# Moving one block's second products behind the first six products of the next pair

## Chip, cores and metric

One core of one Trainium2 chip. The metric is the device time of one execution in microseconds; the kernel before has a median of 809.07 us over 3 runs (808.87 to 809.78).

## What is computed

Three stages, of which the change touches the last. Windowed attention gives x (1536 tokens x 512). A rational feed-forward layer turns it into x again (1536 x 512). Then four experts, each with 1024 hidden units, weighted per token:

```
p = domain_probs / (domain_probs.sum(-1, keepdims=True) + 1e-09)
out = np.zeros((N, D), dtype=np.float32)
for e in range(E):
    h = np.maximum(x @ w1[e], 0.0)
    out += p[:, e:e + 1] * (h @ w2[e])
```

Inputs and output are float32. The output must be close enough to the float32 reference that each product is made from a high and a low half of both factors: three matmuls (high x high, low x high, high x low) for one product.

## The kernel before

**Blocks and pairs.** The 1536 tokens are three blocks of 512. In the last block order they are called PA, PB and LONE (line 818); LONE is the third. The experts' 4 x 1024 hidden units are cut into 16 pairs of two 128-wide tiles, one pair per `Chunk` (line 1006). Each pair has first products (x times w1, up to the relu) and second products (the relu's result times w2, summed into the output).

**First products.** Pair 0 makes them directly: 12 matmuls for each block and tile (`direct`, line 1086). Every later pair makes the six results (three blocks, two tiles) out of 20 products of sums of weight tiles with sums of blocks, three matmuls of 128x512 each (`product`, line 1067, its matmuls at line 1074). The tables `FLOW` and `FLOW_LATE` (lines 63 and 73) list for a pair the order of its steps: `("P", i, bank)` adds product i into a PSUM bank, `("seed", a, b, sign)` has ScalarE copy bank a into a fresh bank b (line 1041), `("spare", a, name)` has ScalarE copy bank a to SBUF (line 327), `("plus", bank, name, sign)` has VectorE add or subtract it (line 1056), and `("gate", bank, tile, block)` takes the relu, with its high half on ScalarE (line 1109) and its low half on VectorE (line 1112). Pair 1 goes by `FLOW_LATE`, whose first steps are

```
    ("P", 18, 0), ("P", 12, 1), ("seed", 0, 2, 1), ("P", 5, 3), ("spare", 1, "A"), ("P", 0, 4), ("seed", 1, 5, 1),
    ("P", 1, 0), ("seed", 3, 6, 1), ("plus", 4, "A", 1), ("P", 7, 0), ("seed", 3, 7, -1), ("spare", 4, "B"),
```

So products 18, 1 and 7 all go into bank 0 (tag `h`), and between 18 and 1 the first seed has to read that bank.

**Second products.** `second` (line 1120) makes, for one pair and block, four groups of 6 matmuls (line 1134), each group in a PSUM bank of tag `acc`, of which there are 4. In pair 0 ScalarE takes each group out into `p`, times the token's probability (line 1152); in the others VectorE adds it to `p` (line 1154). The relu's result is the tile `g` for PA and PB and `gb` for LONE.

**What sets the order.** `emit` first writes down every operation with its engine, an estimate of its time, what it comes after and which buffers it takes or uses. `tick` (line 1209) hands out due times in the order in which `products` (line 1248) is called, and that gives TensorE's operations their place. `Plan.rank` passes due times back to the operations ahead of them, and `Plan.run` lists everything, engine by engine, by when an operation could start and by how late it may be. Each engine then carries out its own list in order, and waits on semaphores where the list says so. For VectorE and ScalarE the place around the change also holds the building of the right factors (`plan_rights`, line 876): sums of blocks (`combine`, line 856), their high halves on ScalarE (line 863) and low halves on VectorE (line 868), in tiles `y`, `z`, `tm`, `w`, `x`.

Before the change the calls at the end of this order are lines 1261 to 1263: pair 0's second products of PA, the direct products of LONE, second products of PB, second products of LONE; then for each later pair its 20 products and the second products of LONE, PB and PA.

Of the kernel before, what the change touches and what calls it, by code (L numbers as in the profile page):

```python
# [20 lines left out]
B, H, S, D, NM = 2, 8, 768, 64, 8  # L21
# [75 lines left out]
FLOWS = (FLOW, BANK, SPARE), (FLOW_LATE, BANK_LATE, SPARE_LATE)  # L97
# [200 lines left out]
def emit(ctx: ExitStack, tc: tile.TileContext, qk, v0, kv, q8, w64, w32, coef, prob, out):  # L298
# [519 lines left out]
    PA, PB, LONE = LAST  # L818
# [429 lines left out]
    def products(c, *todo):  # L1248
        for x in todo:
            chunks[c].order(tick, x)  # L1250

    def a_second():
        t2[ending.pop(0)] = tick(12 * MM)

    lone = ("F", LONE, 0), ("F", LONE, 1)
    for b in (PA, PB):
        for j in range(2):
            products(0, ("F", b, j))
            if ending:
                a_second()  # L1260
    products(0, ("S", PA), *lone, ("S", PB), ("S", LONE))
    for c in range(1, NC):
        products(c, *(x[:2] for x in FLOWS[c == 1][0] if x[0] == "P"), ("S", LONE), ("S", PB), ("S", PA))

    prs = Buf("tm", [128, NT // 128], F32)
    o_ident = add([("POOL", 1.0)], lambda: make_identity(nc, ident))
# [170 lines left out]
```

## Time and profile before

| what | value |
|---|---|
| median of 3 runs | 809.07 us |
| the profiled execution, own time | 810.07 us |
| its span (first to last instruction) | 808.3 us |
| mean granted TensorE clock | 0.997 of full speed |
| TensorE busy | 793.9 us (98%) |
| VectorE, ScalarE, GpSimd busy | 648.9, 487.5, 357.0 us |

The profile is one execution, taken by the hardware profiler. PE is TensorE's matmul, PEld its weight load (which overlaps with matmuls), DVE is VectorE, ACT ScalarE, POOL GpSimd, SPq the queue that issues DMAs. An engine's busy time counts its own instructions, without waits. In the timeline rows that follow each other with the same line and tiles are merged; the time in brackets is how long the engine was idle just before, and what ended it. A matmul's shown end is modelled and reaches over the next one's start, so pace is read from starts.

### The profile page before, as it was taken

How to read it: one execution, taken by the hardware profiler on the slowest of the kernel's cores; microseconds unless marked ns; L12 is line 12 of the kernel's file. 1: busy time of each engine (PE TensorE's matmuls, PEld its weight loads, DVE VectorE, ACT ScalarE, POOL GpSimd, SP SyncE). 2: the span in 40 equal slices, each digit the busy share in tenths (PEclk: the TensorE clock that was granted, in tenths of full speed). 3: DMA queues.
4: the chain of work that ended last, by engine and by line, in shares of the span. 5: the costliest groups of instructions: out<-in, count | busy, mean ns of one | idle time of the engine just before them, and what ended most of it. 6: DMA issues, size and time to landing. Idle time of an engine off the chain costs nothing.

```text
span 808.3 us, 11563 instructions
## 1 busy us (share of the span) xinstructions
PE 793.9 (98%) x4125; PEld 648.0 (80%) x4129; DVE 648.9 (80%) x1018; ACT 487.5 (60%) x1028; POOL 357.0 (44%) x384
## 2 busy tenths in 40 slices
PE   7999999999999999999999999999999999999998
PEld 4667788888888888878888888888888888888886
DVE  5898789999988788879869669669768768768655
ACT  6899878877778777565634534543643643643440
POOL 4698765555567466363434134124224224214100
PEclk9999999999999999999999999999999999999999
DMA  9986132212130100000111011011011001000004
GB/s 346 361 296 204 54 105 79 74 58 75 64 98 7 46 0 2 27 26 27 53 52 50 4 52 53 1 52 53 6 48 53 19 34 52 27 27 0 1 1 156
DMA packets 22057, 55.42 MB, mean 69 GB/s; under 512 B 3952, under 2 KB 4208, under 8 KB 22000
## 3 DMA queue, kind: packets, MB, share of 16 engines
q1 hardware_dynamic: 22000, 54.69, 19.8%
q8 instruction: 32, 0.52, 0.3%
q14 instruction: 25, 0.20, 0.1%
HBM read 51.54 MB, written 3.15 MB: 68 GB/s over the span
## 4 chain that ended last, share of the span: by engine, by line
PE 79%; DVE 8%; ACT 5%; DMA 3%; POOL 2%; issue 2%; SPq 0%; DVEq 0%; POOLq 0%; ACTq 0%
PE acc L1134 31%; PE acc L1074 10%; PE acc L788 10%; PE h L1074 10%; PE h L666 6%; PE att L666 5%; PE att L1074 5%; DMA w<-kv 2%; ACT w L506 2%; DVE ts L745 1%; DVE y L398 1%; DVE tm L733 1%; DMA w<-q 1%; DVE tm L737 1%; DMA w<-qk 1%
## 5 line engine op out<-in xcount | busy, mean ns | idle before, releaser
L1134 PE MATMUL acc<-w,g 128*128 128x512 f32 x762 | 175.5, 389 | 0.0
L1134 PEld LDWEIGHTS acc<-w,g 128*128 128x128 f32 x762 | 143.0, 188 | 29.7
L372 POOL TENSOR_TENSOR w<-stg,w 128x512 fp32r<-128x512 f32 x34 | 44.5, 1328 | 252.7 <-ACT w L327 252.7
L1154 DVE SCALAR_TENSOR_TENSOR p<-acc,pr,p 128x512 f32<-128x512 f32 x179 | 131.2, 744 | 27.8 <-PE acc L1134 25.6
L788 PE MATMUL acc<-g,w 128*128 128x512 f32 x576 | 141.7, 392 | 0.4 <-POOL w L372 0.3
L788 PEld LDWEIGHTS acc<-g,w 128*128 128x128 f32 x576 | 107.0, 188 | 23.7 <-POOL w L372 1.1
L666 PE MATMUL h<-x,w 128*128 128x512 f32 x384 | 95.1, 394 | 0.0
L764 POOL TENSOR_TENSOR ts<-ts,tu 128x512 f32<-128x512 f32 x48 | 63.7, 1328 | 64.5 <-ACT ts L753 63.8
L1134 PE MATMUL acc<-w,gb 128*128 128x512 f32 x384 | 90.2, 390 | 1.8 <-ACT p L1152 1.4
L1134 PEld LDWEIGHTS acc<-w,gb 128*128 128x128 f32 x384 | 71.9, 188 | 17.5 <-ACT p L1152 1.8
L666 PEld LDWEIGHTS h<-x,w 128*128 128x128 f32 x384 | 71.0, 188 | 15.0 <-DVE ts L745 0.2
L1041 ACT ACTIVATE att<-h 128x512 f32<-128x512 f32 x14 | 8.1, 582 | 99.6 <-PE h L1074 99.6
L666 PE MATMUL att<-x,w 128*128 128x512 f32 x264 | 63.4, 389 | 0.0
L1074 PE MATMUL h<-w 128*128 128x512 f32 x222 | 57.9, 390 | 0.0
L666 PEld LDWEIGHTS att<-x,w 128*128 128x128 f32 x264 | 49.6, 188 | 10.3
L863 ACT ACTIVATE w<-z 128x512 fp32r<-128x512 f32 (+1 forms) x45 | 26.8, 598 | 48.2 <-POOL z L856 39.1
L1056 DVE TENSOR_TENSOR att<-att,ts 128x512 f32<-128x512 f32 x45 | 31.5, 699 | 25.9 <-ACT ts L327 24.9
L1074 PE MATMUL acc<-x,w 128*128 128x512 f32 x189 | 50.4, 389 | 0.0
L372 POOL TENSOR_TENSOR w<-y,w 128x512 fp32r<-128x512 f32 x32 | 42.7, 1334 | 17.2 <-ACT w L327 16.3
L1056 DVE TENSOR_TENSOR acc<-acc,ts 128x512 f32<-128x512 f32 x17 | 11.9, 700 | 47.4 <-ACT acc L1041 44.5
L1074 PEld LDWEIGHTS h<-w 128*128 128x128 f32 x222 | 41.6, 188 | 9.0 <-ACT acc L1041 0.4
L372 POOL TENSOR_TENSOR g<-ts,g 128x512 fp32r<-128x512 f32 x28 | 41.2, 1472 | 12.4 <-ACT g L327 12.1
(187 smaller groups left out, 1569.7 us busy)
## 6 DMA issues: line engine op xcount, KB each, us to landing
stg<-w SPq DMA_DIRECT2D x64, 512.0 KB, 3.4
w<-kv SPq DMA_DIRECT2D x32, 256.0 KB, 5.5
w<-q SPq DMA_DIRECT2D x16, 256.0 KB, 5.5
w<-qk SPq DMA_DIRECT2D x8, 400.0 KB, 6.6
out<-p SPq DMA_DIRECT2D x11, 256.0 KB, 2.0
w<-v SPq DMA_DIRECT2D x8, 256.0 KB, 6.4
out<-p SPq DMA_DIRECT2D x2, 128.0 KB, 1.7
pr<-prob SPq DMA_DIRECT2D x1, 24.0 KB, 3.8
```

The source lines that it names most:

```text
L372: engines[op.eng].tensor_tensor(out=dst[:, 1], in0=src, in1=dst[:, 0].bitcast(F32), op=ALU.subtract)
L398: DVE.tensor_scalar(out=y.ap, in0=words(1), scalar1=3, scalar2=0x3FFFFFF8, op0=ALU.logical_shift_left, op1=ALU.bitwise_and,)
L506: ACT.activation(k(n), p1()[:, n * KB : (n + 1) * KB], AF.Exp, scale=SCALE, bias=nm()[:, n : n + 1], accum_out=sm()[:, n : n + 1],)
L666: PE.matmul(s.h.ap, left(a, k), xs[k].ap[:, b], start=(k == 0 and n == 0), stop=(k == KT - 1 and n == 2),)
L764: lambda: POOL.tensor_tensor(out=s.ap, in0=s.ap, in1=u.ap, op=ALU.mult), [ln], [s, u],
L788: PE.matmul(ps, wt[f].ap[:, 1, a, d * 128 : (d + 1) * 128], g.ap[:, b], start=start, stop=stop)
L863: [("ACT", 0.52 * cost)], lambda: ACT.activation(hi(), src(), AF.Copy),
L1041: lambda o, src=src, dst=dst, sign=x[3]: ACT.activation(dst.buf.ap, src.buf.ap, AF.Copy, scale=float(sign)),
L1056: lambda o, ps=ps, s=s, op=ADD if x[3] > 0 else SUB: DVE.tensor_tensor(out=ps.buf.ap, in0=ps.buf.ap, in1=s.buf.ap, op=op),
L1074: PE.matmul(ps.ap, left(a), right(b), start=fresh and n == 0, stop=n == 2, skip_group_check=True,)
L1134: PE.matmul(ps.ap, gs[j][0].ap[:, a, d * 128 : d * 128 + 128], V.ap[:, j, b], start=j == 0 and n == 0, stop=j == 1 and n == 2,)
L1154: DVE.scalar_tensor_tensor(out=y, in0=ps.ap, scalar=p, in1=y, op0=ALU.mult, op1=ALU.add)
```

## The change

Of pair 0's second products, those of LONE are no longer ordered ahead of pair 1's products, but behind the first six of them (18, 12, 5, 0, 1, 7). Nothing else is changed in the text; the other engines' lists are worked out anew from the due times.

```diff
-    products(0, ("S", PA), *lone, ("S", PB), ("S", LONE))
+    products(0, ("S", PA), *lone, ("S", PB))
     for c in range(1, NC):
-        products(c, *(x[:2] for x in FLOWS[c == 1][0] if x[0] == "P"), ("S", LONE), ("S", PB), ("S", PA))
+        firsts = [x[:2] for x in FLOWS[c == 1][0] if x[0] == "P"]
+        if c == 1:
+            products(c, *firsts[:6])
+            products(0, ("S", LONE))
+            firsts = firsts[6:]
+        products(c, *firsts, ("S", LONE), ("S", PB), ("S", PA))
```

TensorE's list where pair 0 ends and pair 1 begins, before (line 1134 are second products, `w,g` of PB, `w,gb` of LONE; line 1074 are pair 1's products):

```order
L1134 MATMUL acc<-w,g 128x512 x24
L1134 MATMUL acc<-w,gb 128x512 x24
L1074 MATMUL h<-w 128x512 x3
L1074 MATMUL acc<-x,w 128x512 x6
L1074 MATMUL h<-w 128x512 x6
L1074 MATMUL h<-x,w 128x512 x3
L1074 MATMUL acc<-x,w 128x512 x6
L1074 MATMUL acc<-w 128x512 x3
```

and with the change:

```order
L1134 MATMUL acc<-w,g 128x512 x24
L1074 MATMUL h<-w 128x512 x3
L1074 MATMUL acc<-x,w 128x512 x6
L1074 MATMUL h<-w 128x512 x6
L1074 MATMUL h<-x,w 128x512 x3
L1134 MATMUL acc<-w,gb 128x512 x12
L1074 MATMUL acc<-w 128x512 x3
L1134 MATMUL acc<-w,gb 128x512 x12
L1074 MATMUL acc<-x,w 128x512 x6
```

The 24 second products of LONE now stand behind 18 matmuls of pair 1, in two halves with product 9 (`acc<-w`) between them; 17 and 3 follow.

The six products in TensorE's changed list more closely, with buffer numbers and the engines waited for (`h_3731` is bank 0, products 18, 1 and 7; `h_3753` is product 0):

```order
L1074 MATMUL h_3731<-w_3465,w_3455 128x512 x3
L1074 MATMUL acc_3738<-x_2815,w_3239 128x512 [waits Activation_49]
L1074 MATMUL acc_3744<-x_2806,w_3239 128x512 [waits Activation_49]
L1074 MATMUL h_3753<-w_3501,w_3239 128x512 [waits DVE_49]
L1074 MATMUL h_3731<-w_3465,w_3455 128x512 [waits Activation_49]
L1074 MATMUL h_3731<-w_3465,w_3455 128x512 [waits Pool_49]
L1074 MATMUL h_3731<-x_3196,w_3455 128x512 x3
L1134 MATMUL acc_3772<-w_2878,gb_3664 128x512 x3
```

The first wait on `h_3731` is product 1's, for the first seed, ScalarE's line 1041.

ScalarE's list at the same place, before (line 863 are high halves of right factors, 1152 evictions of pair 0's second products, 1041 seeds):

```order
L863 ACTIVATE w<-y 128x512 [waits DVE_49]
L863 ACTIVATE x<-y 128x512 [waits DVE_49]
L1152 ACTIVATE p<-acc,pr 128x512 [waits PE_49]
L863 ACTIVATE x<-tm 128x512 [waits DVE_49,Activation_49]
L1152 ACTIVATE p<-acc,pr 128x512 [waits PE_49,Pool_49]
L863 ACTIVATE x<-z 128x512 [waits Activation_49] x2
L1152 ACTIVATE p<-acc,pr 128x512 [waits PE_49] x3
L1041 ACTIVATE acc<-h 128x512 [waits PE_49,Activation_49]
```

and with the change:

```order
L863 ACTIVATE w<-y 128x512 [waits DVE_49]
L863 ACTIVATE x<-y 128x512 [waits DVE_49]
L1152 ACTIVATE p<-acc,pr 128x512 [waits PE_49]
L863 ACTIVATE x<-tm 128x512 [waits DVE_49,Activation_49]
L1041 ACTIVATE acc<-h 128x512 [waits PE_49,Activation_49]
L327 ACTIVATE ts<-acc 128x512 [waits PE_49]
L1041 ACTIVATE att<-acc 128x512 [waits PE_49]
L863 ACTIVATE x<-z 128x512 x2
L327 ACTIVATE tm<-h 128x512 [waits DVE_49]
L1152 ACTIVATE p<-acc,pr 128x512 [waits PE_49,Pool_49]
```

The first seed, `acc<-h`, moves forward from behind all of LONE's evictions to the place behind `x<-tm`; the three high halves and the eviction ahead of it keep their places. On VectorE one addition to `h` (line 1056) moves ahead of two low halves (line 868). GpSimd's and the DMA queue's lists stay as they were.

## Rows read from the trace of the kernel before

**Rows 1.** The page's busy time, share of the span and instructions of each engine.

```profile
PE 793.9 (98%) x4125; PEld 648.0 (80%) x4129; DVE 648.9 (80%) x1018; ACT 487.5 (60%) x1028; POOL 357.0 (44%) x384
```

**Rows 2.** Timeline of TensorE, 342 to 370: start us, length us, what [idle before].

```profile
342.07 5.60 PE L1134 MATMUL acc<-w,g 128*128 128x512 f32 x24
347.51 1.29 PE L1134 MATMUL acc<-w,gb 128*128 128x512 f32 x5
349.24 3.25 PE L1134 MATMUL acc<-w,gb 128*128 128x512 f32 x13 [0.43 <-DVE gb L1112]
353.85 1.66 PE L1134 MATMUL acc<-w,gb 128*128 128x512 f32 x6 [1.37 <-ACT p L1152]
...
357.41 1.77 PE L1074 MATMUL h<-w 128*128 128x512 f32 x6
359.01 0.85 PE L1074 MATMUL h<-x,w 128*128 128x512 f32 x3
...
369.25 3.11 PE L1134 MATMUL acc<-w,gb 128*128 128x512 f32 x13
```

**Rows 3.** Windows: stretch, length, busy PE, PEld, DVE, ACT, POOL, clock, DMA.

```profile
348.00:354.00 6.00, 4.20 (x18) 2.86 (x17) 6.00 (x8) 2.04 (x4) 4.01 (x4) 1.00 0.28 87
369.25:803.00 433.75, 433.75 (x1915) 359.18 (x1914) 329.24 (x490) 197.70 (x369) 129.22 (x150) 1.00 0.11 36
```

**Rows 4.** Chain of waits, 340 to 375: start us, us, what.

```profile
349.19 3.38 DVE y L856 x3
```

**Rows 5.** Timeline of ScalarE, 351 to 358.

```profile
351.45 0.63 ACT L863 ACTIVATE w<-y 128x512 fp32r<-128x512 f32 x1 [4.41 <-DVE y L856]
352.59 0.63 ACT L863 ACTIVATE x<-y 128x512 fp32r<-128x512 f32 x1 [0.51 <-DVE y L856]
353.13 0.67 ACT L1152 ACTIVATE p<-acc,pr 128x512 f32<-128x512 f32 x1
353.70 0.62 ACT L863 ACTIVATE x<-tm 128x512 fp32r<-128x512 f32 x1
354.22 0.68 ACT L1152 ACTIVATE p<-acc,pr 128x512 f32<-128x512 f32 x1
...
357.54 0.61 ACT L1041 ACTIVATE acc<-h 128x512 f32<-128x512 f32 x1
```

**Rows 6.** Timelines of VectorE and GpSimd, 349 to 377.

```profile
349.11 2.31 DVE L856 TENSOR_TENSOR y<-p 128x512 f32<-128x512 f32 x2
351.34 1.22 DVE L856 TENSOR_TENSOR y<-y,p 128x512 f32<-128x512 f32 x1
352.48 0.68 DVE L856 TENSOR_TENSOR tm<-tm,y 128x512 f32<-128x512 f32 x1
...
349.68 2.33 POOL L856 TENSOR_TENSOR z<-stg 128x256 f32<-128x256 f32 x2
...
376.44 1.30 POOL L868 TENSOR_TENSOR w<-z,w 128x512 fp32r<-128x512 f32 x1 [16.45 <-ACT w L863]
```

**Rows 7.** Timeline of TensorE's weight loads, at 358.

```profile
358.21 0.53 PEld L1074 LDWEIGHTS h<-w 128*128 128x128 f32 x3 [0.38 <-ACT acc L1041]
```

**Rows 8.** Windows of 1 us around the two falls of the clock.

```profile
7.00:8.00 1.00, 0.00 (x0) 0.00 (x0) 0.00 (x0) 0.51 (x1) 0.43 (x2) 1.00 0.98 373
8.00:9.00 1.00, 0.83 (x16) 0.79 (x16) 0.39 (x1) 1.00 (x8) 0.40 (x1) 0.71 1.04 409
9.00:10.00 1.00, 1.00 (x19) 0.90 (x16) 0.84 (x3) 1.00 (x8) 0.76 (x5) 0.50 1.02 402
...
11.00:12.00 1.00, 0.82 (x6) 0.44 (x7) 0.48 (x2) 1.00 (x8) 0.92 (x3) 0.59 1.02 410
...
807.00:808.00 1.00, 0.00 (x0) 0.00 (x0) 0.00 (x0) 0.00 (x0) 0.00 (x0) 0.57 0.00 0
```

**Rows 9.** Timeline of TensorE, at 8 and at 803.

```profile
8.17 0.95 PE L490 MATMUL att<-w 128*64 128x64 f32 x16 [1.55 <-ACT w L327]
...
803.08 1.59 PE L1178 MATMUL acc<-w,g 128*128 128x256 f32 x12
```

## The prediction

> **What bounds the kernel.** I read the page first: TensorE is busy 793.9 of 808.3 us, 98% [rows 1], and no other engine is over 80%. So the time is TensorE's matmuls plus the few places where it stands still, and a change of order can only move that standing still. The timeline of TensorE comes next [rows 2]. From 342.07 to 347.51 twenty-four matmuls start 5.44 us apart, so one starts every 0.2267 us. The 24 second products of the third block follow (the row of 347.51 to that of 353.85), then 60 matmuls of the second pair's products, and at 369.25 the next second products. That is 84 matmuls, 84 x 0.2267 = 19.04 us, in 21.74 us: 2.70 us are lost here. Where: five matmuls from 347.51 end their turn at 348.64, the next starts at 349.24 (0.60 us, a wait for VectorE's low half of gb); thirteen from there end theirs at 352.19, the next starts at 353.85 (1.66 us, a wait for ScalarE's eviction); six from 357.41 take 1.60 us instead of 1.36 (0.24 us). The other 0.20 us is spread thin, most of it a slower first step after each stop. Behind that, from 369.25 to 803, TensorE is busy 433.75 of 433.75 us [rows 3]: whatever is won or lost before 369.25 arrives at the end in full.
>
> The chain of waits says who made TensorE stand still: three sums on VectorE, 3.38 us together [rows 4], end at 352.57. ScalarE's rows show how they get to TensorE [rows 5]: ScalarE takes its instructions in the order in which they stand; it stood idle 4.41 us before the copy at 351.45, then began a second copy only at 352.59, when the sums were done; the eviction that TensorE wanted stands behind it and begins at 353.13. So ScalarE was stuck behind VectorE, and the eviction was merely the first thing in its queue that TensorE needed.
>
> **The change, part by part.**
>
> Removed: TensorE no longer asks for the low half of gb at 348.64 nor for the eviction at 352.19. Both stops go, 0.60 + 1.66 us. The low half is ready at 349.2 and the new place needs it far later, so it costs nothing there.
>
> Moved forward: products 18, 12, 5 and 0, twelve matmuls, run from 347.51 to 347.51 + 2.72 = 350.23. What they need is old: their operands were used or made earlier, and the two acc banks come from the evictions that ran before 347.04 (ScalarE is idle for the 4.41 us ahead of 351.45 [rows 5]).
>
> Added: the fifth product, 1, goes into the bank of product 18, and may do so only when ScalarE has copied that bank into the seed of another. In ScalarE's new order this seed stands behind both copies, the eviction and a third copy. None of these four is touched by the change, and what they wait for is VectorE's sums, which don't wait for TensorE's place either: two sums from 349.11 (2.31 us), one from 351.34 (1.22 us), the last from 352.48 (0.68 us) [rows 6]. So they run as before: 351.45, 352.59, 353.13, 353.70, and the seed takes the place at 354.22 where an eviction stood [rows 5]. Before, the seed began at 357.54 [rows 5] and TensorE's weight load for product 1 began at 358.21 [rows 7], 0.67 us later. The same step now gives 354.22 + 0.67 = 354.89. TensorE stands from 350.23 to 354.89: 4.66 us. Four products do not reach across ScalarE's blockade, and the second products that could have filled it (thirteen ran in it before) now stand behind product 1 in TensorE's order.
>
> The rest, 72 matmuls, needs 72 x 0.2267 = 16.32 us. I looked for the next late one. The second of the four groups wants a bank whose last reader is ScalarE's third item behind the seed, done near 356.4, at 357.7; the third group wants a seed behind its first eviction, some 0.6 us to spare; product 17 wants the eviction of the third group, some 0.4 us to spare. All are counted in steps of 0.5 to 0.6 us per ScalarE item, from one start to the next [rows 5], so no second stop, or one of under 0.5 us. With 0.2 us of slow steps as before, 4.66 + 0.20 = 4.86 us are lost, against 2.70: **+2.2 us**.
>
> The clock: this is the term with no row for exactly this case. In the stretch of the old stops the granted clock stayed at 1.00, that is 2.4 GHz [rows 3], with TensorE working between stops of 0.60 and 1.66 us. But the trace has two falls to 0.50, 1.2 GHz [rows 8]. The first: TensorE did nothing from 7 to 8, restarted at 8.17 [rows 9], and the mean of 0.71 from 8 to 9 puts the fall at 8.42. The second: the last matmuls end at 803.08 + 1.59 = 804.67 [rows 9], and the mean of 0.57 from 807 to 808 puts the fall at 807.14, 2.47 us later. The new idle stretch, from the end of the last matmul at about 350.4 to 354.89, is 4.5 us: longer than the idle time ahead of either fall. So I expect one. Its length: low from 8.42 to the middle of 11 to 12 (0.59, so 11.82), 3.40 us [rows 8]; while low, half the work is done. Earliest, 2.47 us into the idle: low from 352.9 to 356.3, of which 1.4 us lie behind the restart, cost 0.7 us. Latest, 0.25 us after the restart as at 8.42: all 3.40 us at half pace, cost 1.7 us. No fall costs 0. I take the middle of the two ends with a fall, **+1.2 us**, and keep 0 and 1.7 for the range.
>
> The rule that bears on this is in the Trainium skill, "TensorE: Matmul & The Clock Gate", section "HAM oscillation — how this bites in real kernels": waits between bursts of matmuls let the clock drop, and each next burst starts slow. By the old stops' rows alone the sum would be +2.2 us; by that rule it is +3.4 us. The two falls in this trace agree with it.
>
> Moved with it, at no cost: on VectorE one addition to h goes ahead of two low halves, which are wanted by products 10 and 16, some forty matmuls (9 us) later; GpSimd's next sums wait for them and start about 1.3 us later, but GpSimd stands idle for 16.45 us behind them [rows 6]. Nothing on the DMA queues moves.
>
> Sum: 2.2 + 1.2 = +3.4 us. The profiled execution took 810.07 us with a span of 808.3, so it would take 813.5; it stands 1.0 us over the median, and on the median of 809.07 the same sum gives **812.5 us**. About 0.2%, 1.6 us, can be told from no change here.
>
> **The rivals.**
> - *The clock holds*: 809.07 + 2.2 = 811.3 us. For it: 1.00 through both old stops. Against it: a fall after 2.47 us of idleness. Chance 0.20.
> - *The other side, the products cover the blockade*: ScalarE makes the seed in its idle 4.41 us. Both old stops and the 0.24 us vanish, with their slow steps 2.7 us: 806.4 us. It decides at about 352.0: a seed that begins 2.2 us before 354.22 leaves the time as it was, an earlier one wins. Right behind the first copy (351.45 + 0.52) would be just even, so the seed must stand ahead of all four. The new order of ScalarE puts it behind them. Chance 0.04.
> - *The blockade is shorter*: if VectorE's three sums took 0.68 us each as the one at 352.48 does, not 1.22 as beside GpSimd's work from 349.68 [rows 6], ScalarE would be free 3 x 0.54 = 1.6 us earlier, and the sum would be +0.6 us without a fall: 809.7 us, no change that can be told. But GpSimd's part in this doesn't move. Chance 0.05.
> - *It gets worse*: a second stop of 0.5 us and a clock that stays low for twice as long (another 1.7 us), because TensorE's restart falls into the low time: near 814.7 us. Chance 0.06.
> - That the change does nothing can be left out: TensorE's new order has the second products moved, only with product 9 between their halves.
>
> **How the numbers follow.** The forecast keeps 0.65, and its own range is 811.9 to 813.0 (fall at its earliest or latest). A range of 8 in 10 takes in the case without a fall and a little scatter of the median, 811.0 to 813.3, and leaves out the second, third and fourth rival, 0.15. Faster by over 0.2%: the second rival, 0.04. Within 0.2%: the third, 0.05, and 0.03 of the first, whose 2.2 us is only 0.6 over the bound: 0.08. Slower: 0.88.
>
> **What the profile would show.** Right: twelve matmuls of L1074 from 347.5, then one stop near 350.2 to 354.9 put down to ScalarE's L1041, the seed near 354.2 just behind a copy of L863, no stop at gb or at L1152, and second products at L1134 from about 356. A granted clock under 1.00 in a few us around 355 shows the clock term, 1.00 throughout refutes it. Wrong: the seed before 352, a stop of under 2.7 us, or a time up to 809.

## The result, and the profile after

The changed kernel takes 813.8 us (median of 6 runs, 812.65 to 814.7), the kernel before 809.01 us beside it (6 runs, 808.8 to 810.62): a ratio of 1.0054, 95% interval 1.0041 to 1.0067. It is slower, and lies 0.5 us above the range of the prediction. The profiled execution took 814.43 us with a span of 812.7 us, 4.4 us more than before; the mean clock is 0.994 where it was 0.997.

The page shows hardly anything: TensorE has the same instructions as in [rows 1] and is busy 1.6 us longer: an instruction at a lower clock counts as busy for longer.

```profile
PE 795.5 (98%) x4125; PEld 650.2 (80%) x4129; DVE 649.2 (80%) x1018; ACT 488.0 (60%) x1028; POOL 355.7 (44%) x384
```

TensorE's timeline in the changed kernel, as in [rows 2] (start us, length us, what, idle before):

```profile
347.27 0.84 PE L1074 MATMUL h<-w 128*128 128x512 f32 x3
347.95 1.52 PE L1074 MATMUL acc<-x,w 128*128 128x512 f32 x6
349.31 0.84 PE L1074 MATMUL h<-w 128*128 128x512 f32 x3
354.60 1.65 PE L1074 MATMUL h<-w 128*128 128x512 f32 x3 [4.45 <-ACT acc L1041]
356.05 1.48 PE L1074 MATMUL h<-x,w 128*128 128x512 f32 x3
357.33 4.18 PE L1134 MATMUL acc<-w,gb 128*128 128x512 f32 x12
361.35 0.85 PE L1074 MATMUL acc<-w 128*128 128x512 f32 x3
...
373.60 2.65 PE L1134 MATMUL acc<-w,gb 128*128 128x512 f32 x11
```

Twelve matmuls (products 18, 12, 5, 0) start from 347.27 on; the turn of the last would end at 347.27 + 12 x 0.2267 = 349.99. Product 1 starts at 354.60. That is one stop of 4.61 us, put down to ScalarE's seed at L1041. Both old stops of [rows 2] are gone. Then something new: from 354.60 to 361.35 stand 18 matmuls, which need 18 x 0.2267 = 4.08 us and take 6.75. They lose 2.67 us without any idle time between them. The 84 matmuls from 347.27 to 373.60 take 26.33 us, 7.29 more than 19.04, and 4.61 + 2.67 is nearly all of it. Before, the same 84 took 21.74 us: 4.59 us less. (The profiled program came to this place 0.24 us earlier than before; its span is 4.4 us longer.)

ScalarE's timeline of the changed kernel shows the queue that made the stop, as in [rows 5]:

```profile
351.20 0.63 ACT L863 ACTIVATE w<-y 128x512 fp32r<-128x512 f32 x1 [4.40 <-DVE y L856]
352.34 0.63 ACT L863 ACTIVATE x<-y 128x512 fp32r<-128x512 f32 x1 [0.50 <-DVE y L856]
352.87 0.67 ACT L1152 ACTIVATE p<-acc,pr 128x512 f32<-128x512 f32 x1
353.44 0.62 ACT L863 ACTIVATE x<-tm 128x512 fp32r<-128x512 f32 x1
353.96 0.58 ACT L1041 ACTIVATE acc<-h 128x512 f32<-128x512 f32 x1
```

The seed could run from about 348 on, when product 18 is in its bank (in an experiment below it begins 0.94 us after the stretch does). ScalarE is idle then, but its list has four other instructions ahead of the seed, and the first waits for VectorE. The chain of waits of the changed kernel has the same three sums as [rows 4], and the seed behind them:

```profile
348.94 3.38 DVE y L856 x3
...
354.06 0.50 ACT acc L1041
```

Why the 18 matmuls lose 2.67 us is in the windows of the changed kernel (columns as in [rows 3]: busy PE, PEld, DVE, ACT, POOL, then the clock):

```profile
353.00:354.00 1.00, 0.00 (x0) 0.00 (x0) 1.00 (x2) 1.00 (x3) 0.00 (x0) 0.60 0.00 0
...
355.00:358.00 3.00, 3.00 (x8) 2.32 (x8) 2.00 (x3) 2.58 (x6) 0.62 (x1) 0.50 0.00 0
358.00:360.00 2.00, 2.00 (x6) 1.52 (x6) 0.00 (x0) 0.00 (x0) 2.00 (x4) 0.50 0.01 4
360.00:361.00 1.00, 1.00 (x6) 0.82 (x5) 0.00 (x0) 0.78 (x2) 1.00 (x3) 0.99 0.00 0
373.60:807.00 433.40, 433.40 (x1914) 358.87 (x1913) 330.34 (x490) 197.82 (x369) 127.98 (x150) 1.00 0.11 36
```

The mean of 0.60 from 353 to 354 is 0.80 us at 0.50 and 0.20 at 1.00, so the clock fell to 1.2 GHz at 353.20, inside the stop, and came back to 2.4 GHz near 360.02 (0.99): 6.82 us of low clock, of which 5.4 lie behind the restart. From 373.60 on TensorE is busy without a gap, so all of it arrives at the end.

### The profile page after: what moved, and what is told of

Same layout as the page of the kernel before. It is cut to its first block, busy times and chain, and to the rows that moved or that the text cites. A ratio compares the mean times of both kernels' runs of the same rounds, so it can differ in the third digit from the quotient of the medians.

```text
span 812.7 us, 11560 instructions
## 1 busy us (share of the span) xinstructions
PE 795.5 (98%) x4125; PEld 650.2 (80%) x4129; DVE 649.2 (80%) x1018; ACT 488.0 (60%) x1028; POOL 355.7 (44%) x384
## 4 chain that ended last, share of the span: by engine, by line
PE 86%; DVE 5%; ACT 4%; POOL 2%; DMA 2%; issue 1%; SPq 0%; DVEq 0%; POOLq 0%; ACTq 0%
PE acc L1134 32%; PE acc L788 13%; PE acc L1074 10%; PE h L1074 10%; PE h L666 8%; PE att L666 7%; PE att L1074 5%; ACT w L506 1%; DMA w<-qk 1%; POOL w L519 1%; DVE y L404 1%; DVE y L410 1%; DMA w<-q 1%; POOL ts L764 0%; ACT w L327 0%
## 5 line engine op out<-in xcount | busy, mean ns | idle before, releaser
L1041 ACT ACTIVATE att<-h 128x512 f32<-128x512 f32 x14 | 8.1, 582 | 99.7 <-PE h L1074 99.7
L863 ACT ACTIVATE w<-z 128x512 fp32r<-128x512 f32 (+1 forms) x45 | 26.8, 599 | 48.1 <-POOL z L856 39.1
```

Source lines behind the costliest of these rows:

```text
L863: [("ACT", 0.52 * cost)], lambda: ACT.activation(hi(), src(), AF.Copy),
```

## The experiments

The first question was how the loss divides between stop and clock, the second what sets the length of the low clock, the third whether ScalarE's order is the cause. Line numbers move by some lines in edited kernels: 1074 becomes 1078, 1084 or 1087, L1041 becomes L1051 or L1054, L863 becomes L864, 1134 becomes 1138, 1144 or 1147, 1152 becomes 1156 or 1162. All medians stand beside the kernel before on the same chip.

**The clock by itself: eighteen matmuls in the stop.** Between products 0 and 1 TensorE makes matmuls into a free bank that nobody reads.

```diff
+                    if c == 1 and x[1] == 0:
+                        keep = bank("att")
...
+                            for _ in range(BUSY):
+                                PE.matmul(keep.ap, left(0), right(0), start=True, stop=True)
```

> The changed kernel with 18 extra matmuls of 128x512 into a free bank between products 0 and 1, so that TensorE works through most of its stop (18 x 0.2267 = 4.1 of 4.5 us); their result is never read. Theory (ScalarE's blockade stops TensorE, and the long idleness then costs clock): the wait for the seed stays, the clock stays at 1.00 around 350 to 360, and the time is the changed kernel's less its clock cost of 2.6 us, about 811.1 us. Rival (the clock is a by-product and what costs is the second products' new place, with their bank waits): the time stays near 813.8, and stops show among the second products.

Measured: 813.22 us against 810.04 us, ratio 1.0033 (1.0020 to 1.0045). By the ratios, 1.0054 and this one, that is 1.7 us less than the changed kernel; expected were 2.6. The stop is filled, and the clock stays up. The timeline of TensorE, then a window:

```profile
350.39 4.24 PE L1044 MATMUL att<-w 128*128 128x512 f32 x18
355.02 0.96 PE L1084 MATMUL h<-w 128*128 128x512 f32 x3 [0.39 <-ACT acc L1051]
...
356.51 3.20 PE L1144 MATMUL acc<-w,gb 128*128 128x512 f32 x12
359.55 0.84 PE L1084 MATMUL acc<-w 128*128 128x512 f32 x3
```

```profile
350.00:361.00 11.00, 10.61 (x46) 8.13 (x45) 7.61 (x10) 7.85 (x14) 5.59 (x8) 1.00 0.14 48
```

Product 1 still waits until the seed is made, so the wait costs the same. Its 18 matmuls now take 355.02 to 359.55, 4.53 us, 0.45 over 4.08: 0.13 at the first step and 0.32 among the twelve second products. So of the 2.67 us that these 18 lost in the changed kernel, 0.45 are lost with the clock up too. The stretch of 84 takes 347.67 to 371.79, 24.12 us. So in the profiles the wait alone costs 24.12 - 21.74 = 2.4 us, and the clock 26.33 - 24.12 = 2.2 us more.

The same kernel was run again beside the changed kernel on one chip:

> The run with 18 extra matmuls in the stop, repeated beside the changed kernel. Theory: the clock holds at 1.00 in the stretch and the time is 1.7 to 2.6 us less than the changed kernel's. Rival (the clock costs nothing there): the same time as the changed kernel.

> The changed kernel, on the same chip as the other two and timed in the same rounds. Theory: about 4.5 us over the kernel before; in its profile one stop of 4.4 to 4.5 us and a low clock that begins inside it.

Measured: 812.62 us with the eighteen matmuls (1.0024, 1.0015 to 1.0032), 814.46 us for the changed kernel (1.0050, 1.0036 to 1.0064), against 810.84 us before. The clock costs 1.8 us in the medians, 2.1 by the ratios. On this chip the changed kernel is 3.6 us slower in the medians (4.1 by the ratio) and not 4.8; its profile has the same stop (4.45 us of idle time), the same low time (6.83 us) and a stretch of 26.22 us. A further profile of the changed kernel has them too:

> The changed kernel once more, for a second profile. Theory: the same stop of 4.4 to 4.5 us behind product 0; the clock falls again, for a time that need not be the 6.83 us of the first profile, and the time differs from 814.4 by half of the difference in low time that TensorE worked in.

Measured: 814.5 us, span 812.7, 4.44 us of idle time, a clock that is low from 353.41 to 360.24.

**Half as many.** The same edit with nine matmuls.

> As the run with 18 extra matmuls, with 9: TensorE works 2.04 us of its stop and then stands idle for about 2.4 us until the seed. Theory: the stop is as long; whether the clock falls is open. If it holds at 1.00, 811.1 us; if it falls as in the changed kernel, about 813.7 us.

Measured: 813.03 us, 1.0040 (1.0026 to 1.0054). TensorE's timeline, then the windows:

```profile
353.97 0.97 PE L1084 MATMUL h<-w 128*128 128x512 f32 x3 [2.44 <-ACT acc L1051]
```

```profile
355.00:356.00 1.00, 1.00 (x5) 0.81 (x4) 0.75 (x2) 1.00 (x3) 0.17 (x1) 0.74 0.00 0
356.00:358.00 2.00, 2.00 (x7) 1.51 (x5) 1.10 (x1) 0.95 (x2) 1.31 (x3) 0.50 0.00 0
358.00:359.00 1.00, 1.00 (x4) 0.80 (x3) 0.00 (x0) 0.69 (x1) 1.00 (x2) 0.55 0.02 8
```

The nine matmuls begin at 349.33 and take 2.20 us. Behind a stop of 2.44 us the clock fell too, but 1.5 us after the restart, at 355.48. It lasted 0.52 + 2 + 0.90 = 3.42 us, half of the changed kernel's. Either the shorter stop or the work during the low time could be the reason; the next two runs part these.

**The same idle time, with and without work behind it.** The unneeded matmuls wait for a copy of ScalarE, so the idle time is in front of them: eight in one kernel, three in the other.

```diff
+    listed.remove(dummy[1])
+    listed.insert(max(map(listed.index, (rights[11][2][0], dummy[0]))) + 1, dummy[1])
```

> The changed kernel, with eight matmuls that are not needed between products 0 and 1, as in the run with nine, but these read the copy that ScalarE begins at 352.3, so they start near 353.0: TensorE stands about 3.0 us, works 1.8 us (twice that at the lower clock), and begins product 1 with hardly a stop more. In the run with nine the idle time came behind them (2.44 us), the clock fell 1.5 us after the restart and was low for 3.41 us; in the changed kernel it fell inside the stop and was low for 6.83 us. Theory: what counts is whether TensorE works while the clock falls and after. Then a fall behind 353.0 is followed by 3.4 us of low clock (cost 1.7 us at most), and the time lies 0.9 us or more under the changed kernel's. Rival: the length of the idle time ahead counts, and 3.0 us is nearer to the changed kernel's 4.45: low for 6.83 us, and the time is that of the changed kernel or above it. No fall at all, with the time of the run with eighteen (1.8 us under the changed kernel), would refute both.

> The same with three matmuls instead of eight, from near 353.0 to 353.7: TensorE stands about 3.0 us, works 0.7 us, and stands another 1.0 to 1.3 us before product 1. By the theory that work while the clock falls makes the low time short, this is in between: 3.4 us if the fall comes while the three or product 1 run, 6.83 us if it comes in the second idle piece. By the rival (the idle time ahead counts) it is as in the run with eight. The stop ahead of product 1 ends at the same time in both, near 354.6 to 355.0.

Measured: with eight 813.88 us, 1.0041 (1.0026 to 1.0056); with three 815.02 us, 1.0052 (1.0036 to 1.0068). TensorE's timeline and windows with eight:

```profile
353.18 3.67 PE L1044 MATMUL att<-x,w 128*128 128x512 f32 x8 [2.87 <-ACT x L864]
356.69 0.85 PE L1084 MATMUL h<-w 128*128 128x512 f32 x3
```

```profile
353.00:354.00 1.00, 0.82 (x2) 0.73 (x3) 1.00 (x3) 1.00 (x3) 0.00 (x0) 0.58 0.00 0
...
356.00:357.00 1.00, 1.00 (x5) 0.82 (x4) 0.75 (x2) 1.00 (x3) 0.38 (x1) 0.71 0.00 0
```

and with three:

```profile
353.42 0.96 PE L1044 MATMUL att<-x,w 128*128 128x512 f32 x3 [2.87 <-ACT x L864]
355.00 1.65 PE L1084 MATMUL h<-w 128*128 128x512 f32 x3 [0.62 <-ACT acc L1051]
```

```profile
354.00:355.00 1.00, 0.38 (x2) 0.00 (x0) 1.00 (x2) 1.00 (x3) 0.00 (x0) 0.66 0.00 0
...
361.00:362.00 1.00, 1.00 (x5) 0.77 (x5) 0.00 (x0) 0.86 (x2) 0.01 (x1) 0.93 0.00 0
```

The idle time is 2.87 us in both. With eight the clock falls at 353.16, just as TensorE restarts, TensorE then works without a gap, and the clock is low for 0.84 + 2 + 0.58 = 3.42 us. With three it falls at 354.32; TensorE stands until 355.00 (0.62 us of idle time), and the clock is low for 0.68 + 6 + 0.14 = 6.82 us. So the idle time ahead did not decide it, and the rival falls: in this stretch the low time was 3.42 us with work all through it and 6.82 us with a stop reaching into it, in one profile each. In the medians the two kernels can't be told apart, as their intervals overlap; the stretches, 25.59 and 26.65 us (to the next second products at 373.01 and 374.32), differ by 1.1 us. The run with eight is only 0.7 us under the changed kernel's 26.33, expected were 0.9 or more: its unneeded matmuls ran at the low clock and held product 1 up until 356.69.

The falls near 8 us, where the first one of [rows 8] stands, don't keep to this. Thirteen of the fourteen profiles have one there, eleven of 3.4 us and two of 6.8, most of their matmuls being smaller ones of 128x64. Two of the runs below contradict each other in it. In the one with four products ahead the clock fell at 7.50, TensorE restarted only at 8.11, and the low time ended at 10.92, after 3.42 us:

```profile
8.11 1.12 PE L490 MATMUL att<-w 128*64 128x64 f32 x16 [2.06 <-ACT w L327]
```

```profile
7.00:8.00 1.00, 0.00 (x0) 0.00 (x0) 0.00 (x0) 0.56 (x2) 0.43 (x2) 0.75 0.98 357
...
10.00:11.00 1.00, 1.00 (x5) 0.22 (x4) 0.51 (x2) 1.00 (x9) 0.92 (x4) 0.54 1.03 410
```

In the one with ScalarE's order alone and TensorE's order of before, TensorE had restarted at 8.27, the clock fell at 9.02 and stayed low until 15.84, 6.82 us, though TensorE stood for only about 0.4 us of it:

```profile
8.27 0.69 PE L490 MATMUL att<-w 128*64 128x64 f32 x16 [1.28 <-ACT w L327]
```

```profile
9.00:10.00 1.00, 0.81 (x16) 0.81 (x16) 0.80 (x4) 1.00 (x9) 0.74 (x4) 0.51 1.02 403
...
15.00:16.00 1.00, 1.00 (x16) 0.67 (x17) 0.51 (x2) 1.00 (x7) 0.97 (x2) 0.58 1.13 428
```

So standing in the low time is not by itself what makes it 6.82 us; what decides between the two lengths in general stays open.

**VectorE's sums shorter.** A tiny GpSimd instruction that reads a late copy holds GpSimd's two sums back, so that they no longer run beside VectorE's.

```diff
+            for y in (a1, a2):
+                y.after.append(tiny)
+                tiny.next.append(y)
```

> The changed kernel, with GpSimd's two sums of 128x256 that run beside VectorE's y sums (349.5 to 351.8) held back until ScalarE's copy x<-tm is made, by a tiny GpSimd instruction that reads that copy. Theory: the y sums take about 0.7 instead of 1.2 us each, ScalarE's copy begins some 1.1 us earlier, the seed with it, and TensorE's stop shrinks from 4.45 to about 3.3 us: at least 1.1 us less than the changed kernel, 812.7 us or, if the clock falls for less time, down to 810.1. Rival (the sums are slow for another reason): 813.8 us, y sums as before.

Measured: 813.54 us, 1.0036 (1.0023 to 1.0049). VectorE's timeline, then TensorE's:

```profile
348.82 1.77 DVE L857 TENSOR_TENSOR y<-p 128x512 f32<-128x512 f32 x2
350.52 0.68 DVE L857 TENSOR_TENSOR y<-y,p 128x512 f32<-128x512 f32 x1
351.13 0.68 DVE L857 TENSOR_TENSOR tm<-tm,y 128x512 f32<-128x512 f32 x1
```

```profile
353.50 1.65 PE L1087 MATMUL h<-w 128*128 128x512 f32 x3 [3.39 <-ACT acc L1054]
```

The sums of 2.31 and 1.22 us in [rows 6] take 1.77 and 0.68 (the first two still begin beside a GpSimd instruction of line 372), ScalarE comes free 1.1 us earlier, and the stop is 1.1 us shorter: the length of ScalarE's blockade is VectorE's sums, as the prediction had it. The clock falls in this stop too and is low for 6.83 us, from 352.68 to 359.51. The stretch takes 25.54 us, 0.8 less than the changed kernel's; the ratio is 1.0036 where the changed kernel has 1.0050 and 1.0054, and the intervals overlap.

**The change with four products ahead instead of six.** Product 1 comes behind the second products again.

```diff
-            products(c, *firsts[:6])
+            products(c, *firsts[:4])
```

> The change with four products moved ahead instead of six: 18, 12, 5, 0, then all second products of the third block, then product 1. Theory: TensorE gets one group of 6 further before it needs the eviction behind ScalarE's blockade, stops near 351.4 until about 353.6, and has one or two short stops behind; idle stretches stay under 2.5 us, the clock stays at 1.00; near 810.3 us, between the kernel before and the changed one. Rival (the second products' place alone): as the changed kernel, near 813.8.

Measured: 812.54 us, 1.0031 (1.0020 to 1.0043): 2.5 us over the 810.04 us beside it, expected were 1.3. The single stop becomes two:

```profile
353.56 1.66 PE L1134 MATMUL acc<-w,gb 128*128 128x512 f32 x6 [2.10 <-ACT p L1152]
357.08 3.02 PE L1134 MATMUL acc<-w,gb 128*128 128x512 f32 x12 [1.86 <-ACT acc L1041]
```

The first waits for the eviction behind the same two copies, the second for a seed further back in the same queue (356.43). The stretch takes 347.21 to 370.82, 23.61 us, 1.87 more than before. In this profile (811.64 us) the clock stayed at 1.00 through both. Other executions had mean clocks down to 0.989 (814.83 us), so a fall there can't be ruled out for them.

**ScalarE's order alone, with the order before.** TensorE's list is that of before; the three copies go behind PB's last eviction.

```diff
+            for i in (13, 11, 15):
+                rights[i][2][0].after.append(o_done[PB, KT - 1])
```

> The kernel before, with TensorE's order as it was, but on ScalarE the last eviction of the second block's second products (line 1152) stands ahead of the copies that wait for VectorE's sums. Theory (ScalarE's order, not TensorE's, makes the stop of 1.66 us): that stop goes, the one of 0.60 us for gb stays, product 1 may wait up to 0.7 us for its seed: 807.3 to 807.8 us. Rival (the stop belongs to the place of the second products in TensorE's order): no change, 809.0 us.

Measured: 809.51 us, 0.9988 (0.9979 to 0.9997). The stop of 1.66 us in [rows 2] is gone, but a smaller one opens at product 1:

```profile
358.01 0.97 PE L1074 MATMUL h<-w 128*128 128x512 f32 x3 [0.60 <-ACT acc L1041]
```

The stretch (348.34 to 369.03) takes 20.69 us, 1.05 less than before. The medians differ by 0.5 us (810.04 to 809.51), the ratio gives 1.0; expected were 1.2 to 1.7.

**ScalarE's order alone, with the changed order.** TensorE's list is that of the change; the three copies go behind the first seed.

```diff
+                    if c == 1 and x[2] == 2:
+                        for i in (13, 11, 15):
+                            rights[i][2][0].after.append(o)
```

> The changed kernel, with TensorE's order as it is, but on ScalarE the three copies of right factors (lines 863: w<-y, x<-y, x<-tm) stand behind the first seed instead of ahead of it. Theory (blockade): the seed is ready near 349, product 1 follows product 0 without a stop, all three stops of the kernel before are gone and no fall of the clock follows: 809.0 - 2.7 = about 806.4 us. Rival (the second products' new place costs by itself): slower than the kernel before by at least 1 us, with a stop that ScalarE's order does not move.

Measured: 808.49 us, 0.9980 (0.9971 to 0.9989). Product 1 no longer waits at all. The gain over the kernel before is 1.6 us, expected were 2.6, since the third group of second products now waits for its seed. ScalarE's timeline, then TensorE's:

```profile
347.37 0.58 ACT L1041 ACTIVATE acc<-h 128x512 f32<-128x512 f32 x1
...
353.70 0.67 ACT L1156 ACTIVATE p<-acc,pr 128x512 f32<-128x512 f32 x1
354.40 0.58 ACT L1041 ACTIVATE acc<-acc 128x512 f32<-128x512 f32 x1
```

```profile
355.04 3.02 PE L1138 MATMUL acc<-w,gb 128*128 128x512 f32 x12 [0.97 <-ACT acc L1041]
```

That seed has an eviction ahead of it, and both stand behind the five copies.

**All of ScalarE's copies behind what TensorE waits for.** To the last edit it adds two: the copies also go behind the first eviction of the second products and the seed that follows it, and one spare copy behind the second eviction.

```diff
+            for i in (13, 11, 15, 10, 16):
+                for o in (out0, self_seed[0]):
+                    rights[i][2][0].after.append(o)
```

> The run with the seed ahead of the copies, and in addition ScalarE's copies of right factors and its copy tm<-h stand behind the first eviction of the third block's second products and the seed that follows it. TensorE's order is that of the changed kernel. Theory (every stop of this stretch is ScalarE's order around VectorE's sums): the remaining stop of 1.25 us before the third group shrinks to under 0.3 us, the eviction itself starting when the last sum that reads its buffer is done, near 352; 1 us less than the seed-first run, about 2.5 us less than the kernel before. Rival (that stop is the price of the second products' new place): it stays at 1 us or more.

Measured: 807.06 us, 0.9957 (0.9944 to 0.9969): faster than both kernels. ScalarE's timeline, then TensorE's windows:

```profile
351.61 0.69 ACT L1162 ACTIVATE p<-acc,pr 128x512 f32<-128x512 f32 x1 [2.38 <-DVE tm L856]
352.33 0.58 ACT L1041 ACTIVATE acc<-acc 128x512 f32<-128x512 f32 x1
...
353.51 0.62 ACT L863 ACTIVATE w<-y 128x512 fp32r<-128x512 f32 x1
```

```profile
345.92:364.96 19.04, 19.04 (x85) 15.77 (x84) 14.86 (x21) 14.87 (x27) 8.28 (x10) 1.00 0.08 28
```

The 84 matmuls take 19.04 us, exactly 84 x 0.2267: no stop, no fall. That is 2.7 us less than before. The medians differ by 3.8 us (3.5 by the ratio). The other 1.1 us don't come from this stretch: it begins at 345.92, not 347.51, and this profile has no low clock from 8 to 12, where [rows 8] has one; no run shows that the edit caused that.

## Why the prediction was right or wrong

**Right: the old stops go, and one new one comes.** Expected was a stop of 4.66 us ahead of product 1, made by the seed in ScalarE's queue; it is 4.61 us. The seed begins 6.69 us after the stretch does, expected were 354.22 - 347.51 = 6.71. VectorE's three sums take 3.38 us as before. With the clock held up by unneeded matmuls the stretch is 2.4 us longer than before, against the +2.2 us of the sum. The second stop, put at nothing or under 0.5 us, shows as 0.32 us while the clock is up; in the changed kernel the low clock hides it. Nothing is lost behind 373.60.

**Wrong: the clock term, "+1.2 us".** That the clock would fall was right. The step that failed is the length of the low clock, 3.40 us, taken from the fall at 8.42 in [rows 8]; it is 6.82 us. At 8.42 TensorE had restarted at 8.17 [rows 9] and worked on, but for a wait of 0.18 us near 11.7; the new fall came inside the stop, 1.40 us ahead of the restart. The prediction did reckon with a fall inside the stop, but gave it the 3.40 us of a fall under work, and so counted 1.4 to 3.4 us of low clock behind the restart where there are 5.4. In this stretch every profile in which TensorE still stands in the low time (the changed kernel three times, the one with shorter sums, the one with three late matmuls) shows 6.8 us; the two in which it works all through show 3.42 us. The falls near 8 us go both ways, so why the clock stayed low for 6.82 us is not settled; that it did, in all three profiles of the changed kernel, is. The term measured 2.2 us in the profiles and 1.8 us in the medians. With 2.2 in place of 1.2 the sum would have been 813.5 us, near the 813.8 us measured.

**Rivals.** The clock holds: refuted, it fell in all three profiles of the changed kernel. The products cover the blockade: refuted for the change, though moving the seed by itself does make product 1's stop vanish. The blockade is shorter: its mechanism is real (1.1 us by holding GpSimd back), but nothing in the change does it. "It gets worse" had the size right, a clock low for twice as long, at a chance of 0.06. Its reason, that the restart falls into the low time, fits this stretch but not the fall at 7.50 above, and it was tied to a second stop that it didn't need.

The Trainium skill ("TensorE: Matmul & The Clock Gate", "HAM oscillation — how this bites in real kernels") says that a wait between bursts makes the next burst start slow, and its example pays 1.67 us of low clock for each wait. The runs agree on the first behind the stops of 3.39 and 4.45 us and one of the two of 2.87; behind the other, and behind 2.44 us, the burst began at the high clock and slowed 0.9 and 1.5 us later, and behind 2.10 and 1.86 us it did not slow. On the length the measurement decides, 3.42 or 6.82 us here.

What stays open besides: the timed runs of the changed kernel spread from 812.65 to 814.7 us, and only profiled ones show a low time. The kernel before spreads as much (808.8 to 810.62 us, and 809.28 to 811.67 on the chip of the second comparison), and a mean clock also holds the fall near 8 us, so the spread doesn't tell whether the low time differs from one execution to the next.

## What to carry to other kernels

When a change takes work away from in front of a wait, look at the other engine's list first: here a seed that could have run 5.7 us earlier stood behind copies which waited for VectorE, and putting ScalarE's instructions in the order in which TensorE wants them turned a loss of 3.6 us into a gain of 3.8 (both on one chip). Price a stop of TensorE with the clock that it may cost: a stop of 4.6 us cost another 1.8 to 2.2 us behind it. Don't take the length of a low clock from a single fall: one trace showed 3.4 us where the next stop had 6.8, so the range has to hold both.

## What the runs showed of the hardware

After a fall, TensorE's clock stayed low for 3.4 or for 6.8 us, in every fall of these profiles whose end lies in the kernel. Among the 128x512 matmuls of this stretch it was 3.42 us where TensorE worked all through the low time (two profiles) and 6.82 us where it still stood for part of it (five profiles; 0.62 us in the one with the least). Near 8 us, among smaller matmuls, 0.61 us of standing came with 3.42 us and about 0.4 us with 6.82, so this is no rule. Idle time ahead did not decide the length (2.87 us led to both), nor is the place of the fall tied to the stop: at 2.44 us of idle time it came 1.5 us after TensorE had restarted. Two stops of 2.10 and 1.86 us with six matmuls between them were followed by no fall in the one profile that has them.

A sum of two 128x512 tiles on VectorE took 0.68 us by itself and about 1.2 us beside GpSimd's sums here: with GpSimd held back the third `y` sum went from 1.22 to 0.68 us, and the first two from 2.31 to 1.77. The Trainium skill ("SBUF — State Buffer", "SBUF: two separate sides") has VectorE and GpSimd take turns at a shared port pair for whole instructions; the rows agree with that, but no run here shows the port itself.
